# Attention with a learned bias and two gated layers: other estimates for the passes that DVE and ACT share

## The chip, the cores and the metric

The kernel runs on one core of a Trainium2 chip. The metric is the device time of one execution in microseconds (us). TensorE (PE) multiplies, VectorE (DVE) and ScalarE (ACT) do the elementwise passes and copy out of PSUM, GpSimd (POOL) issues some loads and does a few subtractions, and SyncE (SP) issues most of the DMA transfers. Each engine takes its instructions in the order of its own list and stops at the first one that still has to wait.

## The reference

```python
# attention: batch 2, heads 8, seq 576, head_dim 64
scores = scale * np.matmul(q, k.transpose(0, 1, 3, 2))
psi_rel = np.log1p(np.abs(rel))                    # rel[i, j] = i - j
psi_i = np.log1p(np.maximum(pos[:, None], 1.0))
x = (psi_rel / psi_i)[..., None]
h = np.maximum(x @ w1 + b1, 0.0)                   # 32 hidden
bias = h @ w2                                      # one value per head, row and column
scores = scores + bias.transpose(2, 0, 1)[None]
attn = softmax(scores)                             # with + 1e-9 in the divisor
x = np.matmul(attn, v)                             # then 1152 tokens x 512
# layer 1, then layer 2 with silu on the first product; 512 -> 1536 -> 512
x = ((x @ w_a) * (x @ w_b)) @ w_out
```

## The kernel before

The program has two stages. In the first, attention, the bias is made by 36 units (u = 0 to 35), each for 16 rows of positions. A unit has four passes `hd` over up to 576 columns (lines 136 on DVE or 138 on ACT), a product with `w2` on PE into a PSUM tile `tp`, and two to four passes `bt` that scale the product into an SBUF tile (line 142 on DVE or 144 on ACT). Then SP writes the tile to a table in DRAM, `bias_d` (line 177). There are five tables, and the attention blocks read them back with shifted rows as `bt` (lines 387 and 384). Units 32 to 35 come first, for the table of block row 4, then units 0 to 7 for the table of block row 0, and so on; the four SBUF tiles of the units are used in turn, so unit 8 can fill its tile only when the write of unit 4 has landed.

Attention goes over 20 steps (a block row t, a pair of heads p), t in the order 4, 0, 1, 2, 3. A step of t = 4 has one half, the others have two, 36 halves in all. For each half PE makes the scores `ps`; DVE adds the bias and finds the row extreme (`es`, line 294); ACT takes the exponential (line 300); PE transposes `es` in three groups of three into `tp`; three copies bring those to SBUF as `ee` (line 305 on DVE, 307 on ACT); PE multiplies by the values into `pu`. The divisors go through `rs`, `rw` and a copy `rc` (line 345 or 347), and line 352 and the two lines 361 and 362 split the result into a rounded and a remaining part, `xh` and `xl`. PE's order in the attention stage is pinned to the order of the program text: scores of half i, transposes of half i - 1, values of half i - 2, then the products of the units that belong to that half.

The second stage is the two layers, with every product made of three PE matmuls (rounded by rounded, remaining by rounded, rounded by remaining). Its weights come as `raw` (line 247), are unpacked on ACT (lines 250, 256) and DVE (lines 251 to 257), and that work begins while attention's last halves run.

Which of DVE and ACT gets a shareable pass or copy is decided while the program is written out. `Share` keeps a sum of estimated time for each of the two engines, and `on_dve` gives a piece to the engine that would then have the smaller sum. The estimates are a fixed part and a slope per column: `DFAST` is DVE's slope for the passes `hd` and the splitting copies of `q` and `k` (line 191 on DVE, 193 on ACT), `DSLOW` its slope for everything that reads PSUM and for the work that is always DVE's. Work that isn't shared is booked as well, but the unpacking of the weights and the second stage are not, and nothing there is shared. Since every decision depends on the sums, one changed estimate moves pieces all along the attention stage. After that a scheduler orders each engine's list by its own model of the times, PE's pinned part excepted, and the orders on SP, DVE and ACT can change with the shares.

Of the kernel before, what the change touches and what calls it, by code (L numbers as in the profile page):

```python
# [35 lines left out]
HDS, BTS, EES = 6, 4, 4  # L36


DFIX, DFAST, DSLOW = 70.0, 0.52, 1.04
AFIX, AELEM = 190.0, 0.86  # L40


# [551 lines left out]
```

## Time and profile before

| | us |
|---|---|
| median of 3 runs (lowest to highest) | 677.38 (673.59 to 678.59) |
| the profiled execution | 677.13 |
| its span in the trace | 675.4 |
| PE busy | 637.3 (94%) |
| DVE busy | 457.6 (68%) |
| ACT busy | 322.4 (48%) |
| granted TensorE clock, mean | 0.986 of full speed |

The span is what the trace covers; 1.7 us of the execution lie around it. Busy shares are averages over stages that have different limits. On DVE and ACT an instruction's record begins before the record of the one ahead of it has ended, so a run of n instructions takes less than n times the mean duration of one.

### The profile page before, as it was taken

Reading aid. Unit: us, or ns where it says so; the run is one execution under the profiler, and the core shown is the slowest. Engines: PE = TensorE matmul, PEld = TensorE weight load, DVE = VectorE, ACT = ScalarE, POOL = GpSimd, SP = SyncE. Lnnn points to the kernel's source line nnn. Section 1 sums busy time; section 2 is a strip of 40 time slices with the busy share of each in tenths; the row PEclk is TensorE's granted clock in tenths of the full one; section 3 lists DMA queues with packets and bytes.
Section 4 is the critical chain, followed back from the end, with each engine's and each line's share of the span. In section 5 each row is a group of like instructions: output and inputs, shape, how many; then the busy total and the mean of one; then the engine's idle time right before and its main releaser. Section 6 shows DMA issues by size and latency. Waiting matters only on the chain.

```text
span 675.4 us, 11776 instructions
## 1 busy us (share of the span) xinstructions
PE 637.3 (94%) x4584; PEld 577.2 (85%) x4584; DVE 457.6 (68%) x1030; ACT 322.4 (48%) x673; POOL 28.3 (4%) x44
## 2 busy tenths in 40 slices
PE   5569899999969999999999999999999999999997
PEld 2246465568858999999999999999999999999997
DVE  6756798888878889999679731699517971521322
ACT  5546777778775574454254321565425531311110
POOL 4000000000000000000000020202000000000000
PEclk8989899999998999999999999999999999999999
DMA  8634554543362353444423400144302420000111
GB/s 325 196 127 157 148 162 138 145 144 116 99 178 81 94 156 126 126 142 141 123 82 136 156 1 1 57 138 141 134 1 80 159 74 1 0 1 1 48 47 48
DMA packets 25096, 71.44 MB, mean 106 GB/s; under 512 B 2672, under 2 KB 4352, under 8 KB 25040
## 3 DMA queue, kind: packets, MB, share of 16 engines
q1 hardware_dynamic: 23008, 63.21, 29.7%
q0 software_dynamic: 2032, 7.47, 3.4%
q8 instruction: 36, 0.59, 0.4%
q14 instruction: 20, 0.16, 0.1%
HBM read 57.42 MB, written 13.25 MB: 105 GB/s over the span
## 4 chain that ended last, share of the span: by engine, by line
PE 83%; DMA 7%; DVE 4%; ACT 3%; issue 1%; SPq 0%; POOL 0%; DVEq 0%; ACTq 0%; POOLq 0%
PE p L460 44%; PE po L460 22%; PE tp L81 8%; PE pu L81 5%; PE ps L81 3%; DMA bias_d<-bt 3%; DMA bt<-bias_d 3%; DMA raw<-in_qd 1%; DVE hd L136 1%; DVE es L294 1%; DMA raw<-in_wm 1%; DVE bt L142 1%; ACT es L300 1%; ACT hd L138 1%; ACT bt L144 1%
## 5 line engine op out<-in xcount | busy, mean ns | idle before, releaser
L481 DVE TENSOR_TENSOR g<-p,g 128x384 f32<-128x384 f32 x72 | 40.0, 555 | 136.2 <-PE p L460 135.9
L460 PE MATMUL po<-gh,wl 128*128 128x384 f32 x288 | 96.5, 335 | 0.0
L460 PE MATMUL p<-xh,wl 128*128 128x384 f32 x288 | 96.4, 335 | 0.0
L460 PE MATMUL p<-yh,wl 128*128 128x384 f32 x288 | 96.4, 335 | 0.0
L460 PE MATMUL p<-xl,wh 128*128 128x384 f32 x288 | 96.4, 335 | 0.0
L460 PE MATMUL p<-yh,wh 128*128 128x384 f32 x288 | 96.3, 335 | 0.0
L460 PE MATMUL po<-gl,wh 128*128 128x384 f32 x288 | 96.3, 335 | 0.0
L460 PE MATMUL p<-yl,wh 128*128 128x384 f32 x288 | 96.3, 334 | 0.0
L460 PE MATMUL p<-xh,wh 128*128 128x384 f32 x288 | 96.2, 335 | 0.0
L460 PE MATMUL po<-gh,wh 128*128 128x384 f32 x288 | 95.4, 335 | 0.0
L480 ACT ACTIVATE g<-p 128x384 f32<-128x384 f32 x72 | 35.4, 492 | 116.2 <-PE p L460 116.0
L483 ACT CAST gh<-g 128x384 fp32r<-128x384 f32 x72 | 36.9, 513 | 81.6 <-DVE g L481 81.6
L81 PE MATMUL tp<-hd,cs 128*32 128x264 f32 (+17 forms) x352 | 51.4, 519 | 16.1 <-DVE hd L136 9.7
L256 ACT CAST wh<-m 128x512 fp32r<-128x512 f32 x72 | 44.3, 621 | 45.8 <-DVE m L255 42.1
L294 DVE CUSTOM_DVE_ANT_0 es<-ps,bt 128x576 f32<-128x576 f32 x72 | 51.7, 751 | 18.5 <-DMA bt<-bias_d 7.5
L300 ACT ACTIVATE es<-es,nm 128x576 f32<-128x576 f32 x72 | 55.6, 773 | 17.2 <-DVE nm L294 16.8
L250 ACT ACTIVATE m<-raw 128x512 f32<-128x512 f32 x72 | 48.4, 677 | 26.5 <-DVE wl L257 18.5
L460 PEld LDWEIGHTS p<-xl,wh 128*128 128x128 f32 x288 | 54.1, 188 | 0.2 <-issue 0.2
L460 PEld LDWEIGHTS p<-xh,wh 128*128 128x128 f32 x288 | 54.0, 188 | 0.2 <-issue 0.2
L460 PEld LDWEIGHTS p<-xh,wl 128*128 128x128 f32 x288 | 54.1, 188 | 0.0
L460 PEld LDWEIGHTS p<-yh,wh 128*128 128x128 f32 x288 | 54.1, 188 | 0.0
L460 PEld LDWEIGHTS po<-gl,wh 128*128 128x128 f32 x288 | 54.1, 188 | 0.0
(67 smaller groups left out, 1107.7 us busy)
## 6 DMA issues: line engine op xcount, KB each, us to landing
raw<-in_wm SPq DMA_DIRECT2D x72, 512.0 KB
bias_d<-bt SPq DMA_DIRECT2D x36, 295.5 KB
bt<-bias_d SPq DMA_DIRECT2D x32, 288.0 KB
vv<-in_vd POOLq DMA_DIRECT2D x4, 640.0 KB, 10.2
kr<-in_kd POOLq DMA_DIRECT2D x4, 576.0 KB, 7.1
bt<-bias_d SPq DMA_DIRECT2D x16, 144.0 KB
out_t<-acc SPq DMA_DIRECT2D x12, 192.0 KB
rawq<-in_qd POOLq DMA_DIRECT2D x16, 128.0 KB, 5.5
```

What stands on the lines that cost most here:

```text
L81: return self.tc.keep_in_program_order(getattr(self.engine, name)(*args, **kwargs))
L136: self.last = self.nc.vector.tensor_scalar(dst, self.LW[:, :n], self.bp[:, m : m + 1], 0.0, op0=ALU.add, op1=ALU.max)
L138: self.nc.scalar.activation(dst, self.LW[:, :n], AF.Relu, bias=self.bp[:, m : m + 1])
L142: self.nc.vector.tensor_scalar(dst, src, self.RE[:, u : u + 1], None, op0=ALU.mult)
L250: nc.scalar.activation(m, hi.bitcast(F32), AF.Abs)
L256: nc.scalar.copy(wh[:, i], m)
L294: nc.vector.tensor_tensor_reduce(out=es[:, j].rearrange("p (a j) -> p a j", a=2), in0=ps[:, j, :, :288], in1=bt[j].rearrange("p (a j) -> p ...
L300: nc.scalar.activation(es[:, j], es[:, j], AF.Exp, bias=nm, scale=-1.0, accum_out=sums[:, j : j + 1])
L460: nc.tensor.matmul(ps, lt, rt, start=first and n == 0, stop=last and n == len(parts) - 1)
L480: nc.scalar.activation(g, pp[0], AF.Silu if layer else AF.Copy)
L481: nc.vector.tensor_tensor(g, pp[1], g, op=ALU.mult)
L483: nc.scalar.copy(gh, g)
```

## The change

Two of the estimates in `Share` are changed: DVE's fixed part and its slope for the fast passes.

```diff
-DFIX, DFAST, DSLOW = 70.0, 0.52, 1.04
+DFIX, DFAST, DSLOW = 160.0, 0.56, 1.04
 AFIX, AELEM = 190.0, 0.86
```

DVE's list goes from 1032 to 997 instructions and ACT's from 603 to 638: 35 pieces change sides, net. By kind these are 12 passes `hd` (98 to 86 on DVE's list), 8 passes `bt` (38 to 30), 11 copies `ee` (50 to 39) and 5 casts of `q` and `k` (12 to 7) from DVE to ACT; of the copies `rc` one more is on DVE (17 to 18). PE's list is the same until 13 matmuls into the second stage; POOL's is the same throughout.

**The first loads.** On SP, the first reads of the table of block row 4 (`bias_d4`) stand behind the four writes of units 32 to 35 and between the writes of units 0 to 3 (`bias_d0`). Before:

```order
L177 DMA bias_d0_57<-bt_306 16x8x591
L387 DMA bt_257<-bias_d4_61 64x1x576 x2
L387 DMA bt_258<-bias_d4_61 64x1x576 x2
L177 DMA bias_d0_57<-bt_321 16x8x591
L177 DMA bias_d0_57<-bt_336 16x8x591
L387 DMA bt_390<-bias_d4_61 64x1x576 x2
L387 DMA bt_391<-bias_d4_61 64x1x576 x2
L177 DMA bias_d0_57<-bt_351 16x8x591
```

Now:

```order
L387 DMA bt_257<-bias_d4_61 64x1x576 x2
L387 DMA bt_258<-bias_d4_61 64x1x576 x2
L387 DMA bt_390<-bias_d4_61 64x1x576 x2
L177 DMA bias_d0_57<-bt_306 16x8x591
L387 DMA bt_391<-bias_d4_61 64x1x576 x2
L387 DMA bt_501<-bias_d4_61 64x1x576
L177 DMA bias_d0_57<-bt_321 16x8x591
```

The write of unit 0 now stands behind six of the loads and not ahead of the first, and the later writes stand between the loads one by one.

On DVE, around the first two `es` (the `ISA` rows of line 294) of the first step, before:

```order
L142 TENSOR_SCALAR bt<-tp,cs 128x47
L136 TENSOR_SCALAR hd<-LW,bp 128x528 x2
L142 TENSOR_SCALAR bt<-tp,cs 128x272
L136 TENSOR_SCALAR hd<-LW,bp 128x512 x2
L195 TENSOR_TENSOR kb<-kr,ka 128x1152
L294 ISA es,nm<-ps,bt 128x576
L294 ISA nm 128x1
L142 TENSOR_SCALAR bt<-tp,cs 128x63
```

Now:

```order
L136 TENSOR_SCALAR hd<-LW,bp 128x560
L136 TENSOR_SCALAR hd<-LW,bp 128x544
L294 ISA es,nm<-ps,bt 128x576
L294 ISA nm 128x1
L136 TENSOR_SCALAR hd<-LW,bp 128x544 x2
L136 TENSOR_SCALAR hd<-LW,bp 128x528
L294 ISA es,nm<-ps,bt 128x576
```

The passes of units 2 and 3 (544 and 528 columns), which stood ahead of the first `es`, now stand behind it.

**Units 7 and 8.** Unit 7 ends the table of block row 0; its passes `bt` have 464 and 127 columns, those of unit 8 have 448 and 143. On DVE before:

```order
L136 TENSOR_SCALAR hd<-LW,bp 128x432 x3
L142 TENSOR_SCALAR bt<-tp,cs 128x448
L136 TENSOR_SCALAR hd<-LW,bp 128x416
L142 TENSOR_SCALAR bt<-tp,cs 128x127
L294 ISA es,nm<-ps,bt 128x576
```

On ACT now:

```order
L138 ACTIVATE hd<-LW,bp 128x448
L144 ACTIVATE bt<-tp,cs 128x464
L144 ACTIVATE bt<-tp,cs 128x127
L138 ACTIVATE hd<-LW,bp 128x432
L338 COPY rw<-rs 128x128
L138 ACTIVATE hd<-LW,bp 128x432
L144 ACTIVATE bt<-tp,cs 128x143
```

The second pass of unit 7 has left DVE, where it stood behind the first pass of unit 8, and follows unit 7's first pass on ACT. On SP the two writes (`bt_594` is unit 7's, `bt_603` unit 8's) stood in this order before:

```order
L177 DMA bias_d0_57<-bt_476 16x8x591
L177 DMA bias_d1_58<-bt_603 16x8x591
L177 DMA bias_d0_57<-bt_594 16x8x591
L384 DMA bt_757<-bias_d0_57 128x1x576
L384 DMA bt_758<-bias_d0_57 128x1x576
```

Now:

```order
L177 DMA bias_d0_57<-bt_476 16x8x591
L177 DMA bias_d0_57<-bt_594 16x8x591
L177 DMA bias_d1_58<-bt_603 16x8x591
L384 DMA bt_757<-bias_d0_57 128x1x576
L384 DMA bt_758<-bias_d0_57 128x1x576
```

Unit 7's write has passed unit 8's, and the loads of block row 0 follow both as before.

**The first weights.** On DVE, where the first weights are unpacked among attention's late halves (line 254 is one of the unpacking passes), the rows around one step's reciprocal (line 336). Before:

```order
L294 ISA nm 128x1
L254 SCALAR_TENSOR_TENSOR m<-raw,m 128x512
L305 COPY ee<-tp 128x384
L336 RECIPROCAL rs<-rs 128x4
L362 TENSOR_TENSOR xl_78<-t_2783,xh_75 128x256
```

Now:

```order
L294 ISA es,nm<-ps,bt 128x576
L294 ISA nm 128x1
L336 RECIPROCAL rs<-rs 128x4
L305 COPY ee<-tp 128x384
L362 TENSOR_TENSOR xl_78<-t_2783,xh_75 128x256
```

The copy `ee` ahead of the reciprocal now stands behind it; of the two copies that stood further up in this stretch one has gone to ACT. On ACT the first unpacking pass of the weights (line 250) keeps its place ahead of an exponential.

## Rows read from the trace of the kernel before

**Rows 1.** Busy time by stage: stretch, length, engines, PE clock, DMA share, GB/s.

```profile
5.00:30.00 25.00, 18.40 (x152) 7.83 (x152) 22.39 (x47) 15.69 (x27) 4.61 (x8) 0.93 0.81 291
30.00:48.00 18.00, 9.17 (x58) 5.13 (x58) 7.86 (x24) 7.99 (x19) 0.00 (x0) 0.81 0.36 128
...
66.00:70.00 4.00, 0.83 (x22) 0.49 (x20) 2.40 (x7) 2.17 (x6) 0.00 (x0) 0.99 0.74 224
70.00:80.00 10.00, 9.58 (x105) 5.59 (x98) 7.92 (x23) 7.09 (x18) 0.54 (x1) 0.83 0.49 125
80.00:140.00 60.00, 57.36 (x583) 35.44 (x582) 53.03 (x153) 46.28 (x111) 2.68 (x5) 1.00 0.53 152
...
190.00:204.00 14.00, 6.89 (x76) 5.27 (x72) 10.64 (x29) 8.86 (x21) 0.00 (x0) 0.97 0.62 177
...
217.00:670.00 453.00, 453.00 (x2640) 452.55 (x2639) 284.19 (x554) 173.97 (x326) 13.20 (x12) 1.00 0.25 81
```

**Rows 2.** The chain that ended last, its transfers: start, us, what.

```profile
17.10 6.54 DMA bias_d<-bt
...
47.91 8.44 DMA bias_d<-bt
...
58.17 3.68 DMA bias_d<-bt
...
62.69 5.55 DMA bt<-bias_d
```

**Rows 3.** Two us of the first loads, columns as in rows 1.

```profile
42.00:44.00 2.00, 1.07 (x8) 0.16 (x8) 0.97 (x3) 0.49 (x2) 0.00 (x0) 1.00 0.26 101
```

**Rows 4.** Timeline of SP: start, us, queue, line, transfer, count.

```profile
25.64 2.47 SPq L387 DMA_DIRECT2D bt<-bias_d  x4
...
57.56 1.16 SPq L177 DMA_DIRECT2D bias_d<-bt  x2
...
62.01 2.62 SPq L384 DMA_DIRECT2D bt<-bias_d  x4
```

**Rows 5.** Timeline around units 7 and 8, DVE, then ACT.

```profile
56.44 0.68 DVE L142 TENSOR_SCALAR bt<-tp,cs 128x448 f32<-128x448 f32 x1 [1.11 <-DMA bias_d<-bt]
...
57.38 0.34 DVE L142 TENSOR_SCALAR bt<-tp,cs 128x127 f32<-128x127 f32 x1
...
54.58 0.63 ACT L144 ACTIVATE bt<-tp,cs 128x464 f32<-128x464 f32 x1
```

**Rows 6.** Timeline around the first load of block row 0, DVE, then PE.

```profile
68.27 0.76 DVE L294 CUSTOM_DVE_ANT_0 es<-ps,bt 128x576 f32<-128x576 f32 x1 [0.97 <-DMA bt<-bias_d]
...
69.56 3.50 PE L81 MATMUL tp<-hd,cs 128*32 128x400 f32 x16 [3.17 <-DVE ee L305]
```

**Rows 7.** Timeline of the first weights, ACT, then DVE.

```profile
193.12 0.66 ACT L250 ACTIVATE m<-raw 128x512 f32<-128x512 f32 x1 [2.74 <-DMA raw<-in_wm]
...
202.94 0.16 DVE L336 RECIPROCAL rs<-rs 128x4 f32<-128x4 f32 x1
```

**Rows 8.** Groups by line and shape: count, busy us, mean ns, idle before.

```profile
L305 DVE COPY ee<-tp 128x384 f32<-128x384 f32 x50 | 26.4, 550 | 2.6 <-PE tp L81 2.6
...
L136 DVE TENSOR_SCALAR hd<-LW,bp 128x528 f32<-128x528 f32 x6 | 2.7, 484 | 0.0
...
L307 ACT COPY ee<-tp 128x384 f32<-128x384 f32 x58 | 27.1, 473 | 13.6 <-PE tp L81 13.4
...
L138 ACT ACTIVATE hd<-LW,bp 128x528 f32<-128x528 f32 x2 | 1.5, 730 | 3.0 <-DVE LW L128 3.0
```

**Rows 9.** Timeline, a run of like passes on DVE.

```profile
44.98 2.03 DVE L136 TENSOR_SCALAR hd<-LW,bp 128x496 f32<-128x496 f32 x5
```

**Rows 10.** Timeline of PE around the second step's scores.

```profile
27.04 1.48 PE L81 MATMUL tp<-hd,cs 128*32 128x264 f32 x12 [0.47 <-DVE hd L136]
36.22 0.85 PE L81 MATMUL ps<-ka,qa 64*128 64x288 f32 x4 [7.70 <-DVE nm L294]
```

**Rows 11.** The page's part on DMA issues: transfer, count, KB each.

```profile
bt<-bias_d SPq DMA_DIRECT2D x16, 144.0 KB
```

## The prediction

> **What bounds the kernel now.** I began with the busy time by stage, to see where time can be won at all. From 217 us to 670 us PE is busy for all of 453 us at the full granted clock [rows 1]; those are the two layers, in which nothing is shared by estimate, so that part only moves forward or back as a block. What the change can touch lies ahead of it, and there PE stands idle in four places: from 5 to 48 us (18.40 of 25 and 9.17 of 18 us busy), from 66 to 70 us (0.83 of 4), thinly from 80 to 140 us (57.36 of 60) and from 190 to 204 us (6.89 of 14) [rows 1]. The span is 675.4 us, and the profiled execution, 677.13 us, is 1.7 us more and all but the median of 677.38 us, so sums made on the trace are made against 677.1.
>
> Next I read the chain of work that ended last for what each of these places waits for. Up to 70 us it is mostly a chain of transfers: writes of the bias table that land 6.54, 8.44 and 3.68 us after their issue, and a load of 5.55 us after the last of them [rows 2]. The first loads read the table of block row 4 and move only 101 GB/s at a DMA share of 0.26 [rows 3], about 4 of the 16 engines; 16 loads of 144 KB [rows 11], 2.36 MB, need 23 us at that rate, and that is what fills 28 to 56 us. At its end the timeline shows a knot. DVE holds the first `bt` pass of unit 8 at 56.44 until the write of unit 4 has landed (1.11 us idle) and only then does the second pass of unit 7, at 57.38 [rows 5]. Unit 7's write goes out at 58.17, lands 3.68 us later at 61.85 [rows 2], and at 62.01 SP issues the first loads of block row 0 [rows 4]. They land at 68.2; DVE has waited 0.97 us for the second of them, and PE, behind a copy `ee` that stands behind that `es` on DVE, 3.17 us [rows 6]. PE's clock is then down for a while: 0.83 on the mean of 70 to 80 us [rows 1], which is 3.4 us at 1.2 GHz. From 80 to 140 us DVE is the fuller of the sharing engines, 53.03 of 60 us against ACT's 46.28 [rows 1]. From 190 us on ACT stands 2.74 us at the first weights' transfer, ahead of an exponential, and then DVE works without a gap up to the reciprocal at 202.94 [rows 7].
>
> **What moves, in engine time.** The 11 copies `ee` take 0.550 us on DVE and 0.473 on ACT [rows 8]: 6.1 us off the one, 5.2 on the other. Twelve `hd` passes, priced by the row of 528 columns at 0.484 and 0.730 [rows 8], are 5.8 off and 8.8 on. The other 12 pieces net, at the copies' price, are 6.6 off and 5.7 on. That is some 18 us off DVE and 20 us on ACT, estimates on the high side, since records overlap: five passes of 496 columns in a row take 2.03 us [rows 9], 0.41 each. Counted along the lists half by half, about 6 off and 8 on fall into the stretch of 80 to 140 us. None of it is on the path by itself, as PE ends everything; it counts where PE waits.
>
> **Units 7 and 8: -2.6 us, between 0 and -3.2.** Unit 7's second pass now follows its first on ACT. The first starts there at 54.58 and takes 0.63 [rows 5]; the second, 127 columns, took 0.34 on DVE and is put at 0.4. So the tile is done at 55.6 and not at 57.7, and its write passes unit 8's on SP. With the same 3.68 us it lands at 59.3. Unit 8's write, the earlier of the two that SP issues from 57.56 [rows 4], keeps its time, so SP is free for the loads at about 58.1 and waits for the landing: 59.4 and not 62.01, 2.6 us sooner. PE can take no more than its 3.17 us of idle time from that. The lower end is a write that queues behind the load stream, as unit 4's did for 8.44 us [rows 2].
>
> **The clock behind that gap: -0.5 us, between 0 and -1.7.** If PE doesn't stop, the 3.4 us at 1.2 GHz would be 1.7 us at 2.4 GHz; but PE is busy only 9.58 of 10 us there [rows 1] and waits for passes, so most of it would be waited off.
>
> **The first loads: -0.5 us, between 0 and -1.6.** The write of unit 0 no longer stands ahead of them. It is 295.5 KB, 1.0 us at the 291 GB/s of that stage [rows 1], and half of the 1.16 us in which SP issues two writes [rows 4], 1.6 in all. But the loads have to wait until the table's own last writes have landed, one of them at 23.64 [rows 2], and SP issues them at 25.64 [rows 4] soon after; the DMA share is 0.81 over 5 to 30 us [rows 1]. I stay near zero.
>
> **80 to 140 us: 0, between -2.6 and +2.1.** DVE goes from 53 to some 47 of 60 us and ACT from 46 to some 54. The fuller engine stays as full, only its name changes. PE's idle time there, 2.64 us, is all that can be won; 8 - 6 = 2.1 us is what the two shifts add together, and bounds the loss.
>
> **The first weights: -1.0 us, between 0 and -1.5.** The wait of ACT for the transfer stays, with its place in the list. Behind it DVE loses two copies ahead of the reciprocal at 202.94, 0.55 us each less an overlap of some 0.06. The reciprocal releases the divisors' copy on ACT and PE's next product. Whatever ACT takes over must fit into its 8.86 busy of 14 us [rows 1].
>
> Sum: -2.6 - 0.5 - 0.5 + 0 - 1.0 = -4.6, so 677.1 - 4.6 = **672.5 us**.
>
> **The rivals.** *The start gives nothing.* The transfers set it, whoever makes the passes: the 23 us of loads stay, and their new neighbours on SP are writes that wait for passes. On DVE the passes of units 2 and 3 now stand behind the first `es`, which waits for the first loads; PE's pinned order has unit 3's products, which went out in a run of 1.48 us at 27.04, ahead of the second step's scores, which started at 36.22 as soon as DVE released them [rows 10]. One pass and these products, 0.48 + 1.48 = 2.0 us, may now lie between, and the 2.6 us are used up. Then only the weights' 1.0 us is left: 676.1 us. For it speaks that these transfers fill the chain up to 70 us; against it, that unit 7's late pass is an order on DVE and no transfer. The Trainium skill's "DMA: Bandwidth & Descriptors" (Why a DMA increments its semaphore by 16 and not by 1) says that a transfer is split over the largest number of engines up to 16 that divides the slowest dimension of both sides, which would be 4 for these 64-row loads; by that rule no order of the lists makes the stream faster, and the trace agrees with its 0.26.
>
> *ACT becomes the bound, and the kernel is slower.* ACT does every exponential, and a copy or a pass put ahead of one delays PE's transposes. From the point at which ACT is as full as DVE was, 0.88 in 80 to 140 us, it has no gaps left to take them in; the estimate is 54 of 60, 0.90. If half of the 8 us it gets there is uncovered, that is +4.0, and with half of the first three terms (-1.8) the time is 679.3 us. For it: the start-to-start time of 0.41 us for 496 columns [rows 9] against 0.438 by the new estimate and 0.328 by the old shows that DVE is now booked too high, by a little; against: the old booking was off by more than twice as much, on the other side. The Trainium skill's "Perfetto Trace Analysis" (Optimizing Scalar/DVE Operations) gives about 60 ns as DVE's own fixed time per instruction on SBUF, which is the old 70 and not the new 160; by it too much would move. The trace's 0.41 us is above what 60 ns and the old slope make, 0.318 us, and I follow the trace.
>
> *Everything gives.* The stretch of 80 to 140 us loses its 2.6 us of idle time too, and the first three terms come at 5.0 instead of 3.6: 677.1 - 5.0 - 2.6 - 1.0 = 668.5 us.
>
> **How the numbers follow.** Forecast 0.50, start gives nothing 0.23, ACT the bound 0.14, everything gives 0.13. The range reaches from just below the last case, 668, to the ACT case, 679.5. The three runs before spread by 0.7%, so 1%, 6.8 us, is about what can be told from no change. Faster by over 1% means below 670.4: the last case and the forecast's lower end, 0.19. Slower by over 1% means above 683.9, for which ACT's part would have to be twice what I gave it: 0.05. Within 1%: 0.76.
>
> **What would show it.** Right: unit 7's write issued before unit 8's, block row 0's loads issued near 59 us, PE's gap at 66 to 70 us gone and its clock up there; DVE near 47 and ACT near 54 us in the stretch that was 80 to 140; the reciprocal of the weights' stretch about 1 us sooner after the first weights; the layers unchanged in length. Wrong: loads of block row 0 still at 62 us (start gives nothing); PE's idle time in the bias stretch above 4 us with ACT named as releaser (ACT the bound). A gap in the two layers would be something that I haven't seen.

## The result and the profile after

The changed kernel takes 670.82 us (median of 8 runs, 669.45 to 673.43) against 677.06 us before (8 runs on the same chip, 673.59 to 678.59): a ratio of 0.9911, 95% interval 0.9885 to 0.9937, or 6.0 us less (4.3 to 7.8). The forecast was 672.5. The profiled execution of the changed kernel took 672.10 us with a span of 670.3, so the pair of traces shows 5.1 us of the gain; the medians lie 1.1 us further apart.

Busy time by stage after, columns as in [rows 1]; the last row is a piece of the two layers.

```profile
5.00:30.00 25.00, 14.32 (x124) 6.61 (x124) 18.18 (x33) 13.85 (x28) 5.33 (x9) 0.84 0.79 294
30.00:48.00 18.00, 17.09 (x142) 8.97 (x144) 12.29 (x35) 14.90 (x34) 0.00 (x0) 0.84 0.48 163
66.00:70.00 4.00, 3.95 (x37) 1.89 (x34) 3.08 (x9) 3.37 (x8) 0.00 (x0) 1.00 0.22 64
70.00:80.00 10.00, 9.66 (x126) 6.36 (x125) 8.37 (x27) 8.68 (x23) 0.54 (x1) 1.00 0.59 166
80.00:140.00 60.00, 58.60 (x602) 37.19 (x604) 51.36 (x144) 52.74 (x126) 3.22 (x6) 1.00 0.53 155
190.00:204.00 14.00, 10.87 (x86) 9.00 (x84) 12.32 (x31) 8.12 (x19) 0.00 (x0) 0.66 0.50 155
217.00:665.00 448.00, 448.00 (x2608) 447.62 (x2608) 282.06 (x549) 170.70 (x320) 13.20 (x12) 1.00 0.25 82
```

Against [rows 1]: PE's gap from 66 to 70 us is gone (3.95 of 4 us busy against 0.83), the granted clock from 70 to 80 us is 1.00 and not 0.83, PE idles 1.40 us in 80 to 140 us and not 2.64, and the layers run without a gap as before. From 190 to 204 us PE is busier than before, but at a granted clock of 0.66 against 0.97.

The chain that ended last, its transfers in the first 70 us (start, us, what):

```profile
18.81 4.62 DMA bias_d<-bt
28.28 11.37 DMA bt<-bias_d
...
51.15 5.49 DMA bias_d<-bt
57.48 5.83 DMA bt<-bias_d
```

Against [rows 2], the write of unit 7 starts at 51.15 and has landed at 56.64; before, it started at 58.17 and had landed at 61.85. It starts 7.0 us sooner and lands 5.2 us sooner, since it now takes 5.49 us and not 3.68. The long write of 8.44 us (unit 4's) is off the chain.

The timeline around units 7 and 8, SP first, then ACT, DVE and PE:

```profile
23.52 3.54 SPq L387 DMA_DIRECT2D bt<-bias_d  x6
...
44.76 11.23 SPq L177 DMA_DIRECT2D bias_d<-bt  x5
56.79 3.01 SPq L384 DMA_DIRECT2D bt<-bias_d  x4
...
50.23 0.89 ACT L144 ACTIVATE bt<-tp,cs 128x464 f32<-128x464 f32 x2
...
54.35 0.68 DVE L142 TENSOR_SCALAR bt<-tp,cs 128x448 f32<-128x448 f32 x1 [2.55 <-DMA bias_d<-bt]
...
64.46 0.33 PE L81 MATMUL tp<-ident,rw 128*128 128x128 f32 x1 [1.50 <-DVE bt L142]
```

Unit 7's two passes follow each other on ACT from 50.23 (the x2), its write is among the five that SP begins at 44.76, and the loads of block row 0 go out at 56.79 and not at 62.01 [rows 4]. DVE still stands at unit 8's first pass for unit 4's write, now for 2.55 us and until 54.35 [rows 5], but nothing that the loads need stands behind it. PE's wait of 3.17 us [rows 6] has become one of 1.50 us, for a pass of a later unit on DVE.

The first weights, in the order ACT, DVE, PE:

```profile
186.95 0.66 ACT L250 ACTIVATE m<-raw 128x512 f32<-128x512 f32 x1 [3.71 <-DMA raw<-in_wm]
...
196.06 0.76 ACT L300 ACTIVATE es<-es,nm 128x576 f32<-128x576 f32 x1
...
196.81 0.39 ACT L338 COPY rw<-rs 128x256 f32<-128x256 f32 x1
...
195.84 0.18 DVE L336 RECIPROCAL rs<-rs 128x4 f32<-128x4 f32 x1
...
188.42 0.76 PE L81 MATMUL tp<-ident,es 128*128 128x128 f32 x5 [3.18 <-ACT es L300]
...
197.26 0.69 PE L81 MATMUL tp<-ident,rw 128*128 128x128 f32 x2 [3.06 <-ACT rw L338]
```

The same copy `rw` and the same two waits of PE before:

```profile
203.14 0.40 ACT L338 COPY rw<-rs 128x256 f32<-128x256 f32 x1 [0.21 <-DVE rs L336]
...
194.59 0.77 PE L81 MATMUL tp<-ident,es 128*128 128x128 f32 x5 [2.44 <-ACT es L300]
...
203.59 0.69 PE L81 MATMUL tp<-ident,rw 128*128 128x128 f32 x2 [3.73 <-ACT rw L338]
```

ACT waits 3.71 us for the raw weights, before 2.74 [rows 7]. The reciprocal comes 8.89 us after ACT's unpacking pass began (195.84 - 186.95), before 9.82 (202.94 - 193.12). The copy `rw` behind it stands after two exponentials on ACT and starts 0.97 us after the reciprocal; before it started at 203.14, 0.20 us after.

A table that the rest of the text uses: the start of the first `es` (line 294) of half 5, which is past the knot of units 7 and 8, and of half 18, with which the bias is done, then the span. The last three columns are the differences of the three parts from the kernel before.

| run | half 5 | half 18 | span | to half 5 | to half 18 | rest |
|---|---|---|---|---|---|---|
| before | 74.24 | 145.47 | 675.4 | | | |
| after | 69.64 | 138.69 | 670.3 | -4.6 | -2.2 | +1.7 |
| e1 new, then old | 69.94 | 147.62 | 679.3 | -4.3 | +6.5 | +1.8 |
| e2 old, then new | 75.04 | 144.22 | 675.3 | +0.8 | -2.1 | +1.2 |
| e3 unit 7's pass alone | 68.43 | 139.13 | 669.6 | -5.8 | -0.5 | +0.5 |
| e4 cast of q alone | 73.42 | 144.67 | 675.6 | -0.8 | 0.0 | +1.0 |
| e5 after, pass put back | 75.77 | 144.82 | 676.2 | +1.5 | -2.2 | +1.5 |
| e6 after, early weights | 72.21 | 141.27 | 668.3 | -2.0 | -2.2 | -2.9 |
| e7 e3, early weights | 69.58 | 140.26 | 667.9 | -4.7 | -0.6 | -2.3 |
| e8 fixed part 300 | 70.14 | 142.06 | 672.5 | -4.1 | +0.7 | +0.5 |
| e9 fixed part alone | 69.12 | 139.46 | 671.4 | -5.1 | -0.9 | +2.0 |
| e10 slope alone | 76.20 | 150.71 | 682.7 | +2.0 | +3.3 | +2.1 |
| e11 e3, spread weights | 68.98 | 139.68 | 663.0 | -5.3 | -0.5 | -6.6 |
| e12 after, spread weights | 71.61 | 140.65 | 663.8 | -2.6 | -2.2 | -6.8 |

These are single executions, and the first part moves from one to the next with the same lists. The first transfer of `q`, issued at 1.99 us, took 7.28 us in the trace of before, 5.40 in that of after and 5.46 in that of e3; in before and e3 the cast of `q` is on DVE, with passes of the first table behind it. The part from half 5 to half 18 hardly moves at all: with the changed lists it took 69.05, 69.05, 69.06 and 69.04 us (after, e5, e6, e12), with the old lists and unit 7's pass early 70.70, 70.68 and 70.70 us (e3, e7, e11).

### The profile page after: what moved, and what is told of

The parts are those of the page before. It is cut to its first block, busy times and chain, and to the rows that moved or that the text cites. A ratio compares the mean times of both kernels' runs of the same rounds, so it can differ in the third digit from the quotient of the medians.

```text
span 670.3 us, 11797 instructions
## 1 busy us (share of the span) xinstructions
PE 637.6 (95%) x4584; PEld 577.9 (86%) x4584; DVE 445.9 (67%) x995; ACT 334.3 (50%) x708; POOL 29.0 (4%) x44
## 4 chain that ended last, share of the span: by engine, by line
PE 84%; DMA 6%; ACT 5%; DVE 2%; issue 2%; SPq 1%; DVEq 0%; ACTq 0%
PE p L460 45%; PE po L460 22%; PE tp L81 8%; PE pu L81 6%; PE ps L81 4%; DMA bt<-bias_d 3%; DMA bias_d<-bt 2%; ACT hd L138 1%; ACT bt L144 1%; DMA raw<-in_wm 1%; ACT es L300 1%; ACT ee L307 1%; SPq L387 1%; DMA LW<-in_lm 0%; DVE hd L136 0%
```

## The experiments

Times are medians; ratios are to the kernel before, run between them on the same chip (676.23 us for e1 to e4, 677.04 for e5 to e8, 676.79 for e9 to e12).

**Half of the change, e1 and e2.** The estimates are switched at half 4, in e1 from new to old and in e2 from old to new. The edit of e1, against the changed kernel (`...` stands for lines left out):

```diff
-        self.spent = [0.0, 0.0]
+        self.spent = [0.0, 0.0]; globals().update(DFIX=160.0, DFAST=0.56)
...
         for i in range(len(halves) + 2):
+            if i == 4: globals().update(DFIX=70.0, DFAST=0.52)
```

> New estimates for halves 0 to 3 and the units written out ahead of them, the old ones from half 4 on. Theory A (the gain is made in the first 65 us, where the write of unit 32 goes out 2.1 us sooner and unit 7's write 7 us sooner, so that the second-block-row scores start 4.9 us sooner; what follows nets out near zero: about -2 us in the bias stretch, +1.8 us at the first weights): the first loads of block row 0 still go out near 57 us and the time is about 672, between 670.5 and 673.5. Rival B (the gain comes from taking passes off DVE all along the bias stretch, 80 to 140 us, and the early start is only waited off later): most of it is gone, 675 to 677.

> The old estimates up to half 3, the new ones from half 4 on: the other half of the change. Theory A: the first loads of block row 0 go out at 62.0 us as before, and the time is 675.5 to 677.5; the bias stretch gives at most the 2 us that it gave with the whole change, and the first weights take part of that back. Rival B: 671 to 673.

Measured: e1 679.39 us, ratio 1.0059 (1.0041 to 1.0077); e2 674.28 us, 0.9983 (0.9969 to 0.9997). The start of e1 is right by theory A, the loads of block row 0 go out at 57.81 and half 5 is 4.3 us early. But 6.5 us are lost by half 18, which neither theory had. The timeline of e1 shows how, DVE first, then ACT and PE:

```profile
95.62 0.74 DVE L294 CUSTOM_DVE_ANT_0 es<-ps,bt 128x576 f32<-128x576 f32 x1
...
96.30 0.75 DVE L294 CUSTOM_DVE_ANT_0 es<-ps,bt 128x576 f32<-128x576 f32 x1
...
96.97 0.17 DVE L336 RECIPROCAL rs<-rs 128x4 f32<-128x4 f32 x1
...
97.34 0.76 ACT L300 ACTIVATE es<-es,nm 128x576 f32<-128x576 f32 x1
...
98.09 0.39 ACT L338 COPY rw<-rs 128x256 f32<-128x256 f32 x1
...
98.54 0.44 PE L81 MATMUL tp<-ident,rw 128*128 128x128 f32 x2 [2.38 <-ACT rw L338]
98.91 2.17 PE L81 MATMUL pu<-ee,vv 128*64 128x128 f32 x20
```

Here a step's reciprocal stands behind the two `es` of the next half on DVE, its copy `rw` then behind both exponentials on ACT, and PE, whose order is pinned, waits 2.38 us for it and makes the values behind it in 2.17 us and not 1.31. After has no such place in this stretch; in e1 it comes twice (at 98.54 and 112.76). So e1 can't be read as the start's worth: the lists after half 4 are neither the old nor the new ones. e2 has its loads at 62.34 us and gains 2.1 us in the bias stretch, as A says, and gives 1.2 back at the weights; its time lies between the two theories, 1.2 us below A's range and 1.3 above B's.

**One pass alone, e3.** The kernel before, with unit 7's second pass on ACT. Nothing else in any list moves but its write.

```diff
-        if self.share.on_dve(n):
+        if self.share.on_dve(n) and (u, n) != (7, 127):
```

> The kernel before with one pass moved and nothing else in any list but the place of its write: unit 7's second pass bt, 127 columns, follows its first on ACT. Theory A: unit 7's write is issued near 55 us, lands near 59.4, the loads of block row 0 go out near 59.5 and not at 62.0, PE's wait of 3.17 us at 66 to 70 us shrinks to below 1, and the time is 674.5 (673.5 to 675.5), or 0.5 us less if the clock stays up at 70 to 80 us. Rival C (the transfers set this place whoever makes the pass: the write queues behind the load stream): loads of block row 0 within 0.7 us of 62.0, time 676.5 to 677.5.

Measured: 672.77 us, ratio 0.9953 (0.9935 to 0.9971), that is 3.2 us less (2.0 to 4.4). The timeline, SP, ACT, DVE, PE:

```profile
56.61 2.89 SPq L384 DMA_DIRECT2D bt<-bias_d  x4
...
52.23 0.88 ACT L144 ACTIVATE bt<-tp,cs 128x464 f32<-128x464 f32 x2
...
54.17 0.68 DVE L142 TENSOR_SCALAR bt<-tp,cs 128x448 f32<-128x448 f32 x1 [1.19 <-DMA bias_d<-bt]
...
61.71 0.76 DVE L294 CUSTOM_DVE_ANT_0 es<-ps,bt 128x576 f32<-128x576 f32 x1
...
63.05 0.76 DVE L294 CUSTOM_DVE_ANT_0 es<-ps,bt 128x576 f32<-128x576 f32 x1 [0.56 <-DMA bt<-bias_d]
...
64.34 2.50 PE L81 MATMUL tp<-hd,cs 128*32 128x400 f32 x16 [0.29 <-DVE ee L305]
```

The loads follow unit 8's waiting pass by 2.44 us (56.61 - 54.17), before by 5.57 (62.01 - 56.44 [rows 4, 5]), and PE's 3.17 us are 0.29. Rival C, by which the transfers set this place whoever makes the pass, is out. The time is 0.7 us below the range that I gave, and the loads went out 2.9 us sooner than I had expected: in this trace the whole start is early (first loads at 23.21 us, before at 25.64), which the pass doesn't cause.

**The cast of q alone, e4.** The kernel before with the first cast of `q` on ACT, behind which, on DVE, the first table's passes had waited.

```diff
-        if self.share.on_dve(w, DFAST):
+        if self.share.on_dve(w, DFAST) and w != 768:
```

> The kernel before with one piece moved, the cast of the first q (768 columns), from DVE, where it waited 1.97 us for the load of q with unit 32's second pass behind it, to ACT. Theory A: the first table write goes out near 9.4 us and not at 11.4, the last of the table's four lands about 2 us sooner, and the first loads go out near 23.6 and not at 25.64; es number 1 starts near 29.2 and not at 31.24. What of this reaches the end: with unit 7's pass still late on DVE behind the wait for unit 4's write, between 0.5 and 2.1 us, time 675 to 676.5. Rival C (the table's own writes set the loads, whatever DVE does): the first loads within 0.5 us of 25.6 and the time 676.5 to 677.5.

Measured: 678.37 us, ratio 1.0041 (1.0026 to 1.0056): slower, where I had expected a small gain. The scheduler answered with other orders in the first 60 us. The first loads went out at 23.00, as expected, but the timeline of DVE shows where they lead:

```profile
53.92 0.68 DVE L142 TENSOR_SCALAR bt<-tp,cs 128x448 f32<-128x448 f32 x1 [1.84 <-DMA bias_d<-bt]
...
54.86 0.34 DVE L142 TENSOR_SCALAR bt<-tp,cs 128x127 f32<-128x127 f32 x1
...
65.06 0.76 DVE L294 CUSTOM_DVE_ANT_0 es<-ps,bt 128x576 f32<-128x576 f32 x1 [3.74 <-DMA bt<-bias_d]
```

Unit 8's pass waits for unit 4's write until 53.92, near e3's 54.17; unit 7's stands behind it, its write takes 4.93 us and not 3.68 [rows 2], and DVE waits 3.74 us for the loads. What the first loads had gained is mostly waited off at this one place, and 0.76 of the clock is granted in 66 to 80 us, before 0.88. The write accounts for some 1.3 us there. In the other traces with the late pass it takes as long as here (4.93 to 5.02 us in e2, e5 and e10), so the 3.68 us of before are the exception. The trace of e4 ends 0.2 us behind that of before, and the rest of the measured loss isn't seen in it.

**The pass put back, e5.** The changed kernel, with unit 7's second pass on DVE again.

```diff
-        if self.share.on_dve(n):
+        if self.share.on_dve(n) or (u == 7 and n == 127):
```

> The changed kernel with one pass put back and nothing else moved but its write: unit 7's second pass bt (127 columns) on DVE again, behind unit 8's first pass, which waits there for the write of unit 4. Theory A (most of the gain hangs on that pass): its write goes out near 55.7 us and not at 51.2, lands near 60, the first loads of block row 0 go out near 60 and not at 56.8, PE idles some 3 us more near 65 us, and the time is 674 (673 to 675.5). Rival C (the other early passes and the balance carry the gain, the single pass is covered by now): 670.5 to 672.

Measured: 678.07 us, ratio 1.0017 (0.9995 to 1.0039). The one pass of 127 columns is worth 7.2 us here (1.0017 / 0.9911 = 1.0107; the two ratios weren't measured side by side, and their intervals together give about 5 to 9.5 us), as much as the whole change or more. Its timeline, DVE and PE:

```profile
54.89 0.68 DVE L142 TENSOR_SCALAR bt<-tp,cs 128x448 f32<-128x448 f32 x1 [2.58 <-DMA bias_d<-bt]
...
55.83 0.34 DVE L142 TENSOR_SCALAR bt<-tp,cs 128x127 f32<-128x127 f32 x1
...
65.99 0.76 DVE L294 CUSTOM_DVE_ANT_0 es<-ps,bt 128x576 f32<-128x576 f32 x1 [4.04 <-DMA bt<-bias_d]
...
69.09 0.48 PE L81 MATMUL tp<-ident,rw 128*128 128x128 f32 x1 [5.34 <-DVE bt L142]
```

The loads go out 6.81 us behind unit 8's pass (61.70 - 54.89). PE's wait is 5.34 us, since with the new lists a pass of a later unit stands ahead of what PE wants next, and the clock granted from 66 to 80 us is 0.77 against 1.00. The time is 2.6 us above theory A's range. At half 5 the trace is 6.1 us behind that of after; 4.9 of it are there when the loads go out (61.70 against 56.79), where theory A had some 3. That the other 1.2 us are that order and the clock is argued and not shown.

**Early weights, e6 and e7.** The first three raw transfers go out one step earlier, on the changed kernel (e6) and on e3 (e7). The function `fetch`, which makes a tile and issues its transfer, and the lines that hand the tile on are left out here.

```diff
-                    if idx == len(steps) - 2:
-                        weights.load(3)
+                    if idx == len(steps) - 3: weights.early = {(0, r): fetch(weights, 0, r) for r in range(3)}
+                    with tc.issue_after(ends[0].ins) if idx == len(steps) - 2 else ExitStack():
+                        weights.load(3 if idx == len(steps) - 2 else 0)
```

> The changed kernel with the first three transfers of raw weights issued one step (7.1 us) earlier on SP, their unpacking kept at about the place that it has on ACT and DVE. Theory A (the first weights' wait takes back part of what the start gave: PE stands 3.18 us for the exponential behind the late transfer, then 3.06 us for a reciprocal behind the unpacking, and the clock falls after each, 1.25 us more than before the change): the wait of 3.71 us on ACT goes, PE's first gap goes, the second shrinks or stays, the clock falls at most once; time 665.5 (663.5 to 667.5). Rival D (the unpacking on DVE, 12 passes, is what holds PE there, and with the transfer early it only holds PE sooner): 669 to 671.

> The kernel before, old estimates, with unit 7's second pass on ACT and the first raw weights issued one step earlier. If the changed estimates are worth nothing beyond that pass, it comes to the time of the changed kernel with early weights, within 1.5 us. If relieving DVE along the attention stage is worth something by itself (1 to 2 us in the trace of the changed kernel), it is 1 to 3 us slower than that one: 667 to 669.

Measured: e6 668.80 us, 0.9873 (0.9841 to 0.9904); e7 669.06 us, 0.9876 (0.9845 to 0.9907). The timeline of e6, ACT and PE:

```profile
189.35 1.23 ACT L250 ACTIVATE m<-raw 128x512 f32<-128x512 f32 x2
...
191.40 0.77 PE L81 MATMUL tp<-ident,es 128*128 128x128 f32 x5 [0.21 <-ACT es L300]
195.66 0.69 PE L81 MATMUL tp<-ident,rw 128*128 128x128 f32 x2 [3.50 <-ACT rw L338]
```

ACT's wait for the transfer is gone and PE's first gap is 0.21 us. The second one stays (3.50 us, a reciprocal behind unpacking on DVE), as rival D says of it: the time is 1.3 us above the upper end of theory A's range and just below D's 669. e7 with the old estimates comes to the same time, 0.3 us apart, as its first theory has it.

**The estimate taken further, e8.** `DFIX` at 300.

> The changed estimate taken further: DVE's fixed part at 300, which moves 22 more instructions from DVE to ACT; unit 7's second pass stays on ACT. For the rival of the prediction in which ACT becomes the bound: in the bias stretch ACT would be near 57 of 60 us busy, PE's idle time there would rise above 4 us with ACT as releaser, and the time would be 674 to 679. If ACT's fullness by itself decides nothing (only which piece stands ahead of which), it stays at 669 to 673.

Measured: 673.35 us, 0.9941 (0.9918 to 0.9964), still faster than before and by the medians 2 to 3 us slower than the changed kernel, though the two intervals overlap. Its bias stretch:

```profile
80.00:140.00 60.00, 56.24 (x587) 36.38 (x587) 44.60 (x128) 56.73 (x135) 3.07 (x6) 1.00 0.50 143
```

ACT is busy 56.73 of 60 us and PE idles 3.76 us, with copies `ee` on ACT named before its waits (0.58 to 0.72 us each, five of them). That is the rival in which ACT becomes the bound, at a fill of 0.95 and at a price of 2.9 us from half 5 to half 18 (71.92 against 69.05), which the traces show. The time lies 0.4 us above the range that I gave for harmless and 0.7 below that for the bound.

**One estimate at a time, e9 and e10.** `DFIX` alone at 160, and `DFAST` alone at 0.56.

> One of the two estimates alone: DVE's fixed part at 160, the slope of the fast passes as before. In the lists 10 passes hd, 7 passes bt and 10 copies ee have left DVE; unit 7's second pass is still on DVE, but unit 8's first pass has gone to ACT, so nothing that waits for unit 4's write stands ahead of it, and its write goes out before unit 8's. Theory A, sharpened (what counts is not the engine but that unit 7's second pass stands behind a pass that waits for a write): loads of block row 0 near 57 us, time 670 to 673.5. Rival C2 (the pass has to be on ACT): loads near 61, time 676 to 679.

> The other estimate alone: the slope of the fast passes at 0.56, the fixed part at 70. Few pieces move (4 passes hd, 2 copies ee to ACT, 2 passes bt the other way); the first loads stand ahead of unit 0's write as in the changed kernel, and unit 7's second pass still follows unit 8's first on DVE. Theory A: loads of block row 0 at 61 to 62 us, PE's idle time near 66 us stays at 3 us or more, time 676 to 679. Rival B (relief of DVE and the order of the first loads carry part of the gain): 673 to 675.5.

Measured: e9 671.78 us, 0.9931 (0.9910 to 0.9952); e10 684.48 us, 1.0114 (1.0091 to 1.0137). The timeline of e9, SP, DVE, ACT:

```profile
58.04 2.72 SPq L384 DMA_DIRECT2D bt<-bias_d  x4
...
53.76 0.34 DVE L142 TENSOR_SCALAR bt<-tp,cs 128x127 f32<-128x127 f32 x1
...
55.56 0.63 ACT L144 ACTIVATE bt<-tp,cs 128x448 f32<-128x448 f32 x1 [1.55 <-DMA bias_d<-bt]
```

Unit 7's pass is on DVE at 53.76 and unit 8's, which waits, on ACT at 55.56; the loads go out 2.48 us behind the latter, and the time lies in theory A's range. So it isn't the engine that counts, but what the pass stands behind. e10 has the loads at 62.92, with unit 7's pass behind unit 8's, 0.9 us later than expected, and is 5.5 us slower than the upper end that I gave: in its table row 2.0 us are lost by the knot (PE waits 4.79 us there), 3.3 in the bias stretch, where one reciprocal stands behind two `es` as in e1 (PE waits 2.38 us for `rw` at 116.57), and 2.1 at the weights.

**Spread weights, e11 and e12.** On e3 and on the changed kernel: the raw transfers three steps earlier, the unpacking one third per step and booked in the sums. Again `fetch` and the lines around it are left out, and the issue at `len(steps) - 2` is gone.

```diff
+                    if idx == len(steps) - 5: weights.early = {(0, r): fetch(weights, 0, r) for r in range(3)}
...
+            if i in (28, 30, 32):
+                with tc.issue_after(ends[0].ins), tc.issue_after(ends[1].ins):
+                    weights.load(1)
+                [share.dve(512) for _ in range(5)], [share.act(512) for _ in range(2)]
```

> The old estimates with unit 7's second pass on ACT, the first raw weights issued three steps earlier than before, and their unpacking spread over three steps (one third each, behind that step's copies, and booked in the shared sums), so that each reciprocal stands ahead of the next third. If what was left at the first weights is the reciprocal behind the unpacking (3.63 us of PE's time) and the clock that falls behind it (about 2 us), the layers begin near 204 us and the time is 663.5 (662 to 666). If the unpacking costs its engine time wherever it stands (7.9 us of DVE, which is 0.85 busy there), PE stands several times for shorter: 667 to 670.

> The changed estimates with the same early weights and spread unpacking. If the changed estimates are worth nothing beyond unit 7's pass, the same as the old ones with that pass, within 1.5 us: 663.5 (662 to 666). If they leave DVE room that the unpacking needs, 1 to 3 us faster than those.

Measured: e11 664.91 us, 0.9827 (0.9803 to 0.9851); e12 664.01 us, 0.9819 (0.9795 to 0.9843): both beat the kernel before and the changed one, and both lie in the range of 662 to 666. Of e12, the stretch by stage:

```profile
190.00:204.00 14.00, 13.00 (x147) 10.76 (x148) 11.46 (x32) 12.07 (x32) 0.00 (x0) 1.00 0.31 114
```

PE is busy for 13.00 of 14 us at the full granted clock, where after had 10.87 at 0.66. The layers begin at 205.45 (204.57 in e11), after at 211.92, before at 217.00. e11 and e12, without and with the changed estimates, are 0.9 us apart, within the 1.5 us that stood for no difference. This fits what I had expected of e11, that what was left at the first weights was the reciprocal behind the unpacking: the part behind half 18 is 6.6 to 6.8 us shorter than before. The earlier issue and the booking weren't tried apart from the spreading.

## Why the prediction was right, step by step

By the pair of traces half 5 came 4.6 us sooner, the stretch from there to half 18 gave 2.2 us more, and the first weights took 1.7 us back; the sum had -3.6, 0 and -1.0. The main term was right in its mechanism and, against this trace, in its size. That the total fits as well as it does is partly luck: two of the other terms were off in opposite directions, and 2.1 of the 4.6 us were there before the first loads went out, in a trace whose transfer of `q` was short. The 4.6 us are made up of 2.1 until the first loads' issue, 0.1 in their stream, 3.0 between its end and the loads of block row 0, and a loss of 0.6 from there to half 5. The medians have 6.0 us, and one trace each can't tell how those divide.

**Units 7 and 8 (-2.6): right.** e3 moves that pass alone and gains 3.2 us (2.0 to 4.4), against 3.1 for this term and the clock's. The step "the loads wait for the landing of unit 7's write" holds in every trace. The loads go out 2.18 to 2.48 us behind unit 8's waiting pass in the nine traces where unit 7's pass is free of it, and 5.57 (before) to 6.90 us (e2) in the five where it isn't. Counted from the landing of the last load of block row 4, that is 3.22 to 3.35 us in the nine, 6.36 in before, and 7.58 to 7.71 in e2, e4, e5 and e10. So the pass costs 3.0 us by the trace of before, within my bound of 3.2, and 4.3 by the other four, above it, since I had the write at the 3.68 us of before.

What I hadn't seen is what takes the pass's place. On SP's queue all these transfers landed in the order of their issue, and the write of unit 7 is the fourth of four behind the load stream. In after the stream's last load lands at 53.46 us and the writes of units 4 to 7 at 54.25, 55.03, 55.81 and 56.64. In the nine traces unit 7's write was issued anywhere from 50.69 to 55.15 us and landed 3.1 to 3.2 us after the last of those loads all the same. So once the pass is free the load stream sets this place, as the rival *the start gives nothing* had it for the whole start; making the pass still sooner gained nothing (issued at 51.15 in after, at 53.14 in e3; the loads go out 2.44 us behind unit 8's pass in both).

**The clock behind them (-0.5): not shown by itself.** The granted clock from 70 to 80 us is up in after and in e3 (1.00), as I had it. From half 5 to half 18 the old lists took 71.23 and 71.26 us with the pass late (before, e4) and 70.68 to 70.70 with it early, but this can't be put down to the clock: in both traces with the late pass it was back at full by 73.4 us, ahead of half 5. What it costs ahead of half 5 isn't told apart from the wait.

**The first loads (-0.5): not shown.** I took the time of the table's last writes as given. But SP issued the first loads 2.1 us sooner in the pair, since the last of those writes landed at 23.43 us and not at 25.55. The transfer of `q` was 1.9 us shorter in this trace, and e3, with old lists and a transfer as short, has its first loads at 23.21, sooner still. Over the traces with old lists from the start (before, e2, e3, e7, e11) the mean is 24.48 us, with the new ones (after, e1, e5, e6, e12) 23.62; the transfer of `q` took 6.78 and 6.04 us on the mean of the same traces, so the lists' share isn't told apart from it. And nothing of it is left further on: the first `es` of block row 0, where unit 7's pass is early, starts at 62.30 on the mean of three old traces (e3, e7, e11) and at 62.26 of four new ones (after, e1, e6, e12). The write of unit 0 has moved from ahead of the loads to between them, and the stream takes as long as before: 30.01 us from the first load's issue to the last one's landing before, 29.94 after, 29.67 to 30.60 over all fourteen traces. The eighth of its sixteen loads is on the chain in both; it took 11.37 us after and, in the chain of before:

```profile
31.30 11.67 DMA bt<-bias_d
```

Two us of the stream after, columns as in [rows 3]:

```profile
42.00:44.00 2.00, 1.84 (x10) 0.29 (x8) 1.72 (x6) 2.00 (x6) 0.00 (x0) 1.00 0.26 102
```

The DMA share is 0.26 as it was [rows 3]. The rule that I drew from the Trainium skill's "DMA: Bandwidth & Descriptors" (Why a DMA increments its semaphore by 16 and not by 1), by which a load of this shape runs on 4 of the 16 engines in any order of the lists, agrees with that.

**80 to 140 us (0): too low.** From half 5 to half 18 the changed lists take 69.05 us against 70.70, so -1.65 us, within my bounds of -2.6 and +2.1. I had DVE near 47 and ACT near 54 us of the 60, the fuller engine as full as before under another name; in the trace both are about equally full (51.36 and 52.74), and PE's small waits for copies `ee` and passes on ACT, six of 0.2 to 0.9 us in the timeline of before, have come down to one of 0.34.

**The first weights (-1.0): wrong sign.** The part behind half 18 took 1.7 us longer. The step itself held: the reciprocal stands 0.93 us nearer to the unpacking, by two copies less on DVE. It failed at "the reciprocal releases the divisors' copy on ACT". The reciprocal now comes right behind the next half's two `es` on DVE, so the copy meets their two exponentials not yet done on ACT and loses 0.77 us of the 0.93 again. That is the order that e1 has in its bias stretch. The raw transfer took 0.74 us longer in this trace (7.02 us against 6.28; 6.3 to 7.4 in the ten traces that issue it at this place), and I had left out the clock, which was at its lower level of 1.2 GHz for 3.4 and then 6.8 us around PE's two gaps (before, 3.4 us around the second). That took 1.25 us more than before, between the release of PE at 197.26 (203.59 before) and the first matmul of the layers. -0.93 + 0.77 + 0.74 + 1.25 = +1.8, and 0.1 us had been gained between half 18 and that place. The other traces with new lists there have +1.2 to +2.0 (e2, e5, e9), those with old ones 0 to +1.0 (before, e3, e4), so about 1 us of it may belong to the lists and the rest to the spread of single executions; e8 with +0.5 and e1, mixed, with +1.8 don't fit that, and it isn't shown.

**The rivals.** *The start gives nothing* is out by e3, though its stream of loads sets the place once the pass is free. *ACT becomes the bound* exists at a fill of 0.95 (e8), where it costs 2.9 us, and not at the 0.88 that ACT has in the changed kernel (52.74 of 60). *Everything gives* came true in part: the stretch of 80 to 140 us gave most of its 2.6 us, the start came to 4.6 of 5.0 only with a short transfer of `q`, and the weights went the other way.

**What stays open** is what the change gives beyond unit 7's pass. Without that pass it gives nothing (e5). With it, the kernels measured side by side differ by 0.3 and 0.9 us (e7 and e6, e11 and e12); the ratios of e3 and after, which weren't, by 0.4%, 2.8 us, and their intervals touch. By parts it is -1.65 in the bias stretch, perhaps +1 at the weights, and +0.6 to +3 us at half 5, where the changed lists have PE wait for a pass of a later unit (1.50 to 1.95 us, with a granted clock from 66 to 80 us of 1.00 in after, 0.83 in e6 and 0.91 in e12). After, e6 and e12 have the same lists up to there, so most of the last range is the spread of one order from one execution to the next.

Whether 160 or 70 is the truer fixed part decided nothing: measured side by side, kernels with either value run within 0.9 us of each other once unit 7's pass is in its place. On it, the prediction read 0.41 us from start to start out of [rows 9], which is the length of the run by five; the starts themselves lie 0.37 to 0.43 us apart, 0.39 on the mean. So the old estimate (0.328) was 0.06 too low and the new one (0.438) is 0.05 too high, nearly as far off. By the Trainium skill's "Perfetto Trace Analysis" (Optimizing Scalar/DVE Operations), with about 60 ns for DVE on SBUF, the old one is nearer; the same sentence has about 125 ns on PSUM, which the copies `ee` and the passes `bt` read, and the prediction left that out.

## What to carry to other kernels

When an estimate reshuffles lists, look for the few places where something that a transfer waits for stands behind an instruction that itself waits for a transfer: one such pass of 0.34 us was worth 3 to 7 us, and the other 34 pieces that moved, net, together at most about 3. Ask too what waits behind it: here the load stream ahead on the same queue set the place as soon as the pass was out of the way. A gain at the start can be given back at a later fixed wait, so price the next wait too, with the copies that stand between the released instruction and the engine that needs it. Small changes of a planner's numbers are a draw of lots unless the lists are read; the draw can also be lost (e1, e10), and spreading the work that makes the late wait (e11, e12) gave more than any estimate tried here.

## What the runs showed of the hardware

The transfers on SP's queue landed in the order of their issue in the first 60 us of all fourteen traces. The first stream, sixteen loads of 144 KB with three or four writes between them, took 29.7 to 30.6 us, whatever the lists. Unit 7's write to the table landed 3.1 to 5.6 us after its issue, and where it was issued ahead of the stream's end (50.69 to 55.15 us) it landed 3.1 to 3.2 us after that end, however early it was issued. The writes of the same size that were issued while the first loads ran took 7.6 to 11.0 us in before and, unit 7's apart, 8.7 to 10.3 in after.

The same first transfer of `q` took 5.40 to 7.28 us from one execution to the next, and the first loads went out between 23.00 and 25.64 us.

After most of PE's waits of 1.8 to 5.3 us in these traces its granted clock was down for the next microseconds (0.5, that is 1.2 GHz; twenty products of values in 2.17 to 2.40 us and not 1.31), but not after each: in e4 a wait of 3.01 us ended at 194.33 and the clock stayed up until 203.03. At the weights this took 1.25 us on top of the waits. At the knot, with the same lists, half 5 starts 12.85 us after the loads of block row 0 go out in after, where PE waited 1.50 us and the clock stayed up, and 15.79 and 14.72 us after it in e6 and e12, where PE waited 1.95 and 1.81 us and the clock was down for 6.8 and 3.4 us.
